# A spectral transformer block on one core: the forward transform's PSUM regions, its order of work and its weight planes rearranged

## The chip, the cores and the metric

The kernel runs on one core of one Trainium2 chip. TensorE (PE, with its weight loads as PEld) multiplies, VectorE (DVE) and ScalarE (ACT) read PSUM and work element by element, GpSimd (POOL) works on SBUF alone, and SyncE (SP) issues nearly all transfers. The metric is the device time of one execution in microseconds (us); the profiled execution has a time of its own and a span, from its first to its last instruction.

## The reference

One adaptive-norm block on x of 2048 tokens by 640 channels, bf16, batch 1:

```
mod = (silu(c) @ w_mod)                       # six rows of 640: sa ca ga sb cb gb
h = layernorm(x) * (1 + ca) + sa
x = x + ga * irfft2(rfft2(h) * (w_r + 1j*w_i))    # over tokens and channels
h = layernorm(x) * (1 + cb) + sb
x = x + gb * ((silu(h @ w_gate) * (h @ w_up)) @ w_down)   # hidden width 1728
```

## The kernel before

The 2D transform is done by matmuls. A token is 16p + t, with p one of 128 partitions and t one of 16 tiles; a channel is 5a + r, with r one of 5. The program has three parts, each with an order of steps written out as a string of short names; every engine runs its instructions in the order in which these steps issue them, and a scheduler adds only the waits. Tiles in PSUM come from pools of numbered buffers; a pool's next tile waits for the last reader of the buffer it takes. PSUM has eight banks, 512 fp32 columns each.

**Forward pass** (pool `ps1`, the plan "T0 T1 h0 ..."). For each of the 16 tiles: T transposes x in five 128x128 pieces into `t1ps` (L268); h copies them to `hT_all`, a ring of HB = 6 in SBUF (L271, on ACT but for tile 0); G multiplies each piece with itself and with two constant columns (+1/128, -1/128), so that the diagonal holds the sum of squares and two more columns hold the mean and its negative, in columns 320:450 of `t1ps` (L276); d reads those on DVE (L282 and its accumulator, then v, L284); m copies the negative mean to `negm` on ACT (L287); p and r make the reciprocal root for two tiles (L291 ACT, L295 DVE); s scales the token table Gtab by it (L300, L301, POOL; tile 15 on DVE); B multiplies `hT_all` with the channel table Rs into `zps` (L306); Z adds the mean's share, rv times `negm`, and copies to SBUF (L312, DVE); S multiplies Z with the scaled token table, four matmuls into `aps` (L320, L321); A copies that to `A_sb` (L327, ACT). `t1ps` has two buffers of one bank, `zps` one buffer of two banks, `aps` two of two banks. Ahead of this, `mod_ca` makes 1 + ca (25 one-column matmuls, L221, and an add, L337), which scales Rp into Rs (L341 on DVE for r = 0, 2, 4; L345 on ACT for 1, 3); rv is the column sum of Rs (L352) times 0.2 (L356, ACT). At its end `ms`, `sacs`, `mh`, `sh` make the transform of sa as `dsa` (L372 to L393).

**Middle stage** (pool `ps2`, four buffers of two banks, the plan "B4 B6 L0 Jn ..."). `A_sb` is cut in 17 units. Units 0 to 3 and 16 are transposed by TensorE (t2 L436, copy_t L442), the others by a DMA transpose on SP (L429, from B4 on). For each unit: X (stage_x, L456 to L464) is the short transform over the 16 tiles and the 5 channel residues, in which two matmuls of 5 rows, `first` with `dsa` (L459), add the share of sa; Xe copies it (L471, ACT); P multiplies with the spectral weights (L489, DVE, two instructions); Y transposes the products back (L503, L507) and y copies (L514, ACT or DVE); E is the inverse short transform (L530 to L538) and e copies to `Ep` (L548). The weights must be had in reversed order as well. For w_i this is a DRAM copy, `Wneg`, written by four DMAs (L198 to L201) and read back into `Wq` (L204). For w_r TensorE does it in two halves (turn_w: `jrev` L592, and the rows that wrap round by one-row matmuls of `identb`, L594), copied by ACT (L597). Jn, W and m negate parts on DVE (L254). `ga`, `gt`, `cb`, `sb` make the other rows of the modulation (L221 on PE); ga is spread over the partitions through DRAM (L236, L242) and multiplied into `Rinv_sb` (Ri, L585); L0 to L5 issue the later weights' DMAs (L602 to L616; Wu in L4, Wg in L5).

**Late stage.** The inverse pass (va L669, VT L676, dinv L682, x1 L685), the second norm, and the feed-forward (gu L774 and L761, silu L779, product L783, down projection L875 and L862, output L889).

Of the kernel before, what the change touches and what calls it, by code (L numbers as in the profile page):

```python
# [22 lines left out]
NC5 = 5  # L23
# [81 lines left out]
def adaln_block_kernel(  # L105
# [30 lines left out]
    one_p_ca = const.tile([P, NR], F32, name="one_p_ca")  # L136
# [5 lines left out]
    ssq, v25, rstd1, negm = (const.tile([P, NT], F32, name=n) for n in ("ssq", "v25", "rstd1", "negm"))  # L142
# [5 lines left out]
    dsa = const.tile([NR, 2, NR, 68], BF16, name="dsa")  # L148
    first = const.tile([NR, 128], BF16, name="first")
# [5 lines left out]
    HB = 6  # L155
# [20 lines left out]
    Wneg = dram.tile([P, NT, 2, 64], BF16, name="Wneg")  # L176
# [10 lines left out]
    nc.sync.dma_start(wm_ca, wm_v[:, :, D:2 * D])  # L187
    nc.sync.dma_start(Rp, R_dram)
    nc.sync.dma_start(x_sb[:, 2:4, :], x_v[:, 2:4, :])
    nc.sync.dma_start(Gtab[:, 0:4], G_dram[:, 0:4])  # L190

    for g in range(1, 4):
        nc.sync.dma_start(x_sb[:, 4 * g:4 * g + 4, :], x_v[:, 4 * g:4 * g + 4, :])
        nc.sync.dma_start(Gtab[:, 4 * g:4 * g + 4], G_dram[:, 4 * g:4 * g + 4])
    wv = A_w_i.rearrange("(k2 k1) l -> k2 k1 l", k1=P)[:, :, 64:320]
    to = Wneg[:].rearrange("k1 k2 m l -> k2 k1 m l")
    for m in range(2):
        nc.sync.dma_start(to[:, 1:128, m], wv[:, 127:0:-1, 128 * m:128 * m + 64])  # L198
    w0 = wv[:, 0].rearrange("k2 (m l) -> k2 m l", m=2)[:, :, 0:64]
    nc.sync.dma_start(to[0:15, 0], w0[1:16])  # L200
    nc.sync.dma_start(to[15:16, 0], w0[0:1])  # L201
    nc.sync.dma_start(wm_sa, wm_v[:, :, 0:D])
    nc.sync.dma_start(Wb[:, 0, :, 0:321], A_w_i.rearrange("(k2 k1) l -> k1 k2 l", k1=P))
    nc.sync.dma_start(Wqp[:, 2], Wneg[:].rearrange("k1 k2 m l -> k1 (k2 m l)"))  # L204
    nc.sync.dma_start(Ktab[:], K_dram)
    nc.sync.dma_start(Wb[:, 1, :, 0:321], A_w_r.rearrange("(k2 k1) l -> k1 k2 l", k1=P))
    nc.sync.dma_start(KIt[:], KI_dram)
    nc.gpsimd.memset(identb[:], 0.0)
# [4 lines left out]
                            pattern=[[1, 128]], channel_multiplier=1)  # L213
    nc.gpsimd.memset(first[:], 0.0)
    nc.gpsimd.memset(first[:, 0:1], float(S))
# [42 lines left out]
    with tc.tile_pool(name="ph1", bufs=3) as ph1, \  # L258
         tc.tile_pool(name="ps1", bufs=2, space=bass.MemoryType.PSUM) as ps1:
        t1s, zs, Zs, apss, Gss = {}, {}, {}, {}, {}  # L260
        ones = ph1.tile([P, 128], BF16, name="ones", bufs=1)
        nc.gpsimd.memset(ones[:], 1.0)

        def turn(t):
            t1s[t] = ps1.tile([P, 512], F32, name="t1ps", tag="t1")
            h = t1s[t][:, 0:320].bitcast(BF16).rearrange("p (r q) -> p r q", r=NR)
            for r in range(NR):
                nc.tensor.transpose(h[:, r, :], x_sb[:, t, r::NR], identb[:])  # L268

        def turned(t):  # L270
            (nc.vector.tensor_copy if t in HT_DVE else nc.scalar.copy)(  # L271
                hT_all[:, t % HB, :, 0:128], t1s[t][:, 0:320].bitcast(BF16).rearrange("p (r q) -> p r q", r=NR))

        def sums(t):
            for r in range(NR):
                nc.tensor.matmul(t1s[t][:, 320:450], lhsT=hT_all[:, t % HB, r, 0:128], rhs=hT_all[:, t % HB, r, 0:130],  # L276
                                 start=(r == 0), stop=(r == NR - 1))

        def stats(t):
            g = t1s[t][:, 320:450]  # L280
            junk = ph1.tile([P, 128], BF16, name="junk", bufs=2)
            nc.vector.tensor_tensor_reduce(out=junk[:], in0=g[:, 0:128], in1=identb[:], scale=25.0 / D, scalar=25.0 * EPS,  # L282
                                           op0=ALU.mult, op1=ALU.add, accum_out=ssq[:, t:t + 1])
            nc.vector.scalar_tensor_tensor(v25[:, t:t + 1], g[:, 128:129], g[:, 129:130], ssq[:, t:t + 1], ALU.mult, ALU.add)  # L284

        def mean(t):
            nc.scalar.copy(negm[:, t:t + 1], t1s[t][:, 449:450])  # L287
# [9 lines left out]
        def gscale(t):  # L297
            Gss[t] = ph1.tile([P, 3, 128], BF16, name="Gs", bufs=5)
            e = nc.vector if t in S_DVE else nc.gpsimd
            e.tensor_scalar(Gss[t][:, 0:2], Gtab[:, t], rstd1[:, t:t + 1], None, ALU.mult)  # L300
            e.tensor_scalar(Gss[t][:, 2], Gtab[:, t, 1], rstd1[:, t:t + 1], -1.0, ALU.mult, ALU.mult)  # L301

        def dfwd(t):
            zs[t] = ps1.tile([P, 2, 512], F32, name="zps", tag="z", bufs=1)
            for r in range(NR):
                nc.tensor.matmul(zs[t][:, r // 4, 128 * (r % 4):128 * (r % 4) + 128], lhsT=hT_all[:, t % HB, r, 0:128], rhs=Rs[:, r, :],  # L306
                                 start=True, stop=True)

        def zcopy(t):
            Zs[t] = ph1.tile([P, NR, 128], BF16, name="Z", bufs=4)  # L310
            z = zs.pop(t)
            nc.vector.scalar_tensor_tensor(Zs[t][:].rearrange("p r q -> p (r q)"), rv, negm[:, t:t + 1],  # L312
                                           z[:].rearrange("p b q -> p (b q)")[:, 0:D], ALU.mult, ALU.add)

        def s1(t):
            Z, Gs = Zs.pop(t), Gss.pop(t)
            apss[t] = ps1.tile([P, 2, 512], F32, name="aps", tag="a")
            for cc, a, b in ((0, 0, 2), (1, 1, 0)):
                o = apss[t][:, cc, 0:325].rearrange("p (r l) -> p r l", r=NR)
# [3 lines left out]
        def acopy(t):  # L323
            ap = apss.pop(t)
            o = A_sb[:, :, t, :, :]
            i = ap[:, :, 0:325].rearrange("p c (r l) -> p l c r", r=NR)
            (nc.vector.tensor_copy if t in A_DVE else nc.scalar.copy)(o, i)  # L327

        mpss = []

        def mod_ca(_):
            mpsA = ps1.tile([P, 2, 512], F32, name="mpsA", tag="a")
            mod_cols(mpsA[:, 0], wm_ca, strided=True)
            mpss.append(mpsA)

        def one_ca(_):
            nc.vector.tensor_scalar_add(one_p_ca[:], mpss[0][:, 0, 0:NR], 1.0)  # L337

        def rs_dve(_):
            for r in (0, 2, 4):  # L340
                nc.vector.tensor_scalar_mul(Rs[:, r, :], Rp[:, r, :], one_p_ca[:, r:r + 1])  # L341

        def rs_act(_):
            for r in (1, 3):
                nc.scalar.activation(Rs[:, r, :], Rp[:, r, :], ACT.Copy, scale=one_p_ca[:, r:r + 1])  # L345

        rvs = []

        def rv_mm(_):
            rvs.append(ps1.tile([P, 2, 512], F32, name="rvps", tag="a"))  # L350
            for b, w in ((0, 4), (1, 1)):
                nc.tensor.matmul(rvs[0][:, b, 0:128 * w], lhsT=ones[:], rhs=Rs[:, 4 * b:4 * b + w, :].rearrange("p r q -> p (r q)"),  # L352
                                 start=True, stop=True)

        def rv_out(_):
            nc.scalar.activation(rv, rvs[0][:].rearrange("p b q -> p (b q)")[:, 0:D], ACT.Copy, scale=0.2)  # L356

        cps = ps1.tile([P, 512], F32, name="cps", tag="t1")
        for k in range(NC5):
            nc.tensor.matmul(cps[:, k:k + 1], lhsT=c_row[0:1, k * 128:(k + 1) * 128], rhs=one11[:], start=True, stop=True)  # L360
        keep_warm(ps1, "t1", 12)
        nc.scalar.activation(sc_f[:], cps[:, 0:NC5], ACT.Silu)
# [3 lines left out]
        mps = []  # L366

        def mod_sa(q):
            if q == 0:
                mps.append(ps1.tile([P, 512], F32, name="mpsB", tag="t1"))  # L370
            for k in range(NC5):
                nc.tensor.matmul(mps[0][:, q:q + 1], lhsT=wm_sa[:, k, q:D:NR], rhs=sc_col[:, k:k + 1],  # L372
                                 start=(k == 0), stop=(k == NC5 - 1))

        def sa_cs(_):
            nc.vector.tensor_tensor(sacs[:], cs_v, mps[0][:, 0:NR].unsqueeze(2).to_broadcast([P, NR, 25]), ALU.mult)

        def mod_sahat(_):
            mps.append(ps1.tile([P, 512], F32, name="sps", tag="t1"))
            sv = sacs[:].rearrange("p r (f m) -> p r f m", f=5)  # L380
            for cc, a, b, e in ((0, 0, 1, 3), (1, 2, 0, 4)):
                o = mps[1][0:NR, 128 * cc:128 * cc + NL]
# [7 lines left out]
        def sa_out(_):  # L390
            sh = mps[1][0:NR, 0:256].rearrange("p (c l) -> p c l", c=2)[:, :, 0:NL].unsqueeze(2).to_broadcast([NR, 2, NR, NL])
            e5 = identb[0:NR, 0:NR].unsqueeze(1).unsqueeze(3).to_broadcast([NR, 2, NR, NL])
            nc.vector.tensor_tensor(dsa[:, :, :, 0:NL], sh, e5, ALU.mult)  # L393

        HT_DVE, A_DVE, S_DVE = (0,), (), (15,)
        GROUP = {0: 1, 1: 2, 3: 2, 5: 2, 7: 2, 9: 2, 11: 2, 13: 2, 15: 1}
        plan = (
            "T0 T1 h0 h1 G0 G1 d0 ca m0 d1 p0 r0 m1 oc rsD T2 rsA T3 h2 s0 rvp rv B0 h3 G2 G3 Z0 d2 B1 m2 p1 r1 d3 s1 m3 S0 "
            "T4 Z1 h4 G4 A0 T5 d4 s2 B2 h5 S1 Z2 m4 p3 G5 A1 T6 r3 d5 B3 s3 h6 S2 Z3 m5 G6 A2 T7 s4 d6 B4 h7 S3 Z4 m6 p5 G7 "
            "A3 T8 r5 d7 B5 s5 h8 S4 Z5 m7 G8 A4 T9 s6 d8 B6 h9 S5 Z6 m8 p7 G9 A5 T10 r7 d9 B7 s7 h10 S6 Z7 m9 G10 A6 T11 "  # L400
            "s8 d10 B8 h11 S7 Z8 m10 p9 G11 A7 T12 r9 d11 B9 s9 h12 S8 Z9 m11 G12 A8 T13 s10 d12 B10 h13 S9 Z10 m12 p11 G13 "
            "A9 T14 r11 d13 B11 s11 h14 S10 Z11 m13 G14 A10 T15 s12 d14 B12 h15 S11 Z12 m14 ms0 p13 G15 A11 ms1 r13 B13 d15 "
            "s13 ms2 ms3 Z13 m15 ms4 p15 S12 sacs s14 B14 r15 A12 s15 mh Z14 S13 B15 A13 S14 Z15 A14 S15 A15 sh "
        )
        steps = {"ca": mod_ca, "oc": one_ca, "rsD": rs_dve, "rsA": rs_act, "rvp": rv_mm, "rv": rv_out, "T": turn, "h": turned, "G": sums,
# [558 lines left out]
```

## Time and profile before

| | us |
|---|---|
| median of 3 runs | 281.07 (280.49 to 281.20) |
| the profiled execution, its own time | 280.74 |
| its span | 279.0 |
| PE busy | 266.0 (95%) |
| DVE busy | 149.8 (54%) |
| ACT busy | 125.2 (45%) |
| POOL busy | 21.2 (8%) |
| forward pass ends (last copy to `A_sb`) | 37.72 |
| inverse pass starts (first `va` matmul) | 79.25 |

Times in timelines and chains count from the span's start. A row of a timeline is: start, duration, engine, line, operation, result and operands, shape, count, and in brackets how long the engine had been idle and what ended that. Matmuls are pipelined, so a row's duration contains a tail that the next matmul overlaps: five 128-column matmuls in a row hold PE for about 0.28 us and read as 0.44.

### The profile page before, as it was taken

What the parts mean: (1) busy time and instruction counts of PE and PEld (TensorE: products, weight loads), DVE (VectorE), ACT (ScalarE), POOL (GpSimd) and SP (SyncE); (2) the same over time, 40 slices, a digit from 0 to 9 for tenths busy, and PEclk for the clock granted to TensorE, in tenths of its full rate; (3) what the DMA queues carried; (4) which work ended last, traced back from release to release, by engine and by line L of the source; (5) the groups of instructions that cost most, each with busy time, mean ns of one, the idle gap of its engine ahead of it and who ended that gap; (6) DMA issues with size and microseconds to landing.
All of it is one profiled execution on the core that took longest, in us unless ns stands there. A gap on an engine that the chain in (4) does not pass through costs nothing.

```text
span 279.0 us, 5360 instructions
## 1 busy us (share of the span) xinstructions
PE 266.0 (95%) x2191; PEld 166.3 (60%) x2191; DVE 149.8 (54%) x356; ACT 125.2 (45%) x239; POOL 21.2 (8%) x42
## 2 busy tenths in 40 slices
PE   6899989999996999999999999999999999999994
PEld 5677845787886665446654445664444674444663
DVE  2588856867858667896434534432325253422151
ACT  5699676877669996723022222203223203223000
POOL 2477710000000000000000000000000000000000
PEclk9999999999999999999999999999999999999999
DMA  7979949965599201005110004011002211000011
GB/s 248 356 151 362 308 82 197 329 210 178 175 318 367 74 9 34 1 0 96 47 56 5 9 0 94 12 61 33 12 0 40 57 71 33 12 0 0 0 49 47
DMA packets 38559, 28.84 MB, mean 103 GB/s; under 512 B 22022, under 2 KB 35591, under 8 KB 38407
## 3 DMA queue, kind: packets, MB, share of 16 engines
q1 hardware_dynamic: 38533, 28.50, 35.3%
q8 instruction: 17, 0.28, 0.4%
q14 instruction: 7, 0.06, 0.1%
q10 hardware_dynamic: 2, 0.00, 0.0%
HBM read 21.42 MB, written 3.15 MB: 88 GB/s over the span
## 4 chain that ended last, share of the span: by engine, by line
PE 83%; ACT 6%; DVE 4%; DMA 3%; issue 1%; SPq 0%; ACTq 0%; DVEq 0%
PE gu L774 40%; PE oa L875 20%; ACT early L271 3%; PE yps L503 2%; PE t1ps L276 2%; DMA x_sb<-in_A_x_dram 2%; PE va L669 2%; PE t1ps L268 2%; PE gu L761 2%; DVE late L685 1%; DMA ga_bc<-ga_row 1%; PE m_ps L221 1%; PE oa L862 1%; DVE PP L489 1%; PE oab L682 1%
## 5 line engine op out<-in xcount | busy, mean ns | idle before, releaser
L783 DVE TENSOR_TENSOR AT<-gu,sg 128x512 bf16<-128x512 f32 x52 | 35.9, 690 | 53.9 <-ACT sg L779 53.9
L774 PE MATMUL gu<-h2T_all,Wg 128*128 128x512 bf16 x260 | 64.6, 379 | 0.0
L774 PE MATMUL gu<-h2T_all,Wu 128*128 128x512 bf16 x260 | 64.6, 379 | 0.0
L779 ACT ACTIVATE sg<-gu 128x512 f32<-128x512 f32 x52 | 31.0, 596 | 70.1 <-PE gu L774 68.5
L875 PE MATMUL oa<-late,AT 128*128 128x320 bf16 x403 | 56.1, 299 | 0.0
L875 PEld LDWEIGHTS <-AT 128*128 128x128 bf16 x429 | 40.8, 98 | 17.2 <-issue 1.4
L774 PEld LDWEIGHTS <-Wu 128*128 128x128 bf16 x260 | 25.4, 98 | 30.7
L774 PEld LDWEIGHTS <-Wg 128*128 128x128 bf16 x260 | 25.1, 98 | 29.3
L889 DVE TENSOR_TENSOR xo<-oa,late 128x320 bf16<-128x320 f32 x31 | 20.0, 695 | 29.5 <-PE oa L862 16.3
L685 DVE SCALAR_TENSOR_TENSOR late<-oab,x_sb 128x640 bf16<-128x640 f32 x16 | 14.0, 884 | 9.4 <-PE oab L682 9.1
L763 ACT ACTIVATE sg<-gu 64x512 f32<-64x512 f32 x4 | 2.3, 586 | 34.9 <-PE gu L761 34.9
L312 DVE SCALAR_TENSOR_TENSOR Z<-rtile,negm,zps 128x640 bf16<-128x640 f32 x16 | 14.0, 876 | 2.6 <-ACT rtile L356 1.8
L300 POOL TENSOR_SCALAR Gs<-Gtab,rstd 128x256 bf16<-128x256 bf16 x15 | 13.8, 923 | 12.9 <-DMA Gtab<-tab_G 7.4
L693 ACT ACTIVATE junk<-late,mean 128x640 bf16<-128x640 bf16 x16 | 13.2, 827 | 0.3
L471 ACT CAST X<-xps 128x640 bf16<-128x640 f32 x16 | 11.2, 698 | 3.7 <-PE xps L464 2.5
L327 ACT CAST A_sb<-aps 128x650 bf16<-128x650 f32 x16 | 11.2, 702 | 2.6 <-PE aps L321 2.3
L503 PE MATMUL yps<-identb,PP 128*128 128x128 bf16 x130 | 10.2, 220 | 1.6 <-DVE PP L489 1.6
L669 PE MATMUL va<-Htab,Ep 128*128 128x128 bf16 x160 | 10.7, 219 | 0.7 <-ACT VT L676 0.4
L271 ACT COPY early<-t1ps 128x640 bf16<-128x640 bf16 x15 | 10.4, 692 | 1.9 <-PE t1ps L268 0.9
L676 ACT CAST VT<-va 128x640 bf16<-128x640 f32 x16 | 10.4, 700 | 1.4 <-PE va L669 1.4
L489 DVE TENSOR_TENSOR PP<-X,Wq 128x512 bf16<-128x512 bf16 x16 | 9.2, 575 | 2.5 <-ACT Wq L597 2.5
L669 PEld LDWEIGHTS <-Ep 128*128 128x128 bf16 x160 | 9.9, 118 | 0.9 <-issue 0.6
(288 smaller groups left out, 334.3 us busy)
## 6 DMA issues: line engine op xcount, KB each, us to landing
out_dram<-xo SPq DMA_DIRECT2D x15, 160.0 KB, 1.8
Wu<-in_B_w_up_dram SPq DMA_DIRECT2D x1, 2080.0 KB, 8.9
late<-in_B_w_down_dram SPq DMA_DIRECT2D x1, 2080.0 KB
x_sb<-in_A_x_dram SPq DMA_DIRECT2D x3, 640.0 KB, 9.6
early<-in_w_mod_dram SPq DMA_DIRECT2D x2, 800.0 KB, 4.8
wm_g<-in_w_mod_dram SPq DMA_DIRECT2D x2, 800.0 KB, 7.0
Wb<-in_A_w_i_dram SPq DMA_DIRECT2D x1, 1284.0 KB
Wb<-in_A_w_r_dram SPq DMA_DIRECT2D x1, 1284.0 KB, 10.7
```

What stands on the lines that cost most here:

```text
L271: (nc.vector.tensor_copy if t in HT_DVE else nc.scalar.copy)(hT_all[:, t % HB, :, 0:128], t1s[t][:, 0:320].bitcast(BF16).rearrange("p (r q ...
L300: e.tensor_scalar(Gss[t][:, 0:2], Gtab[:, t], rstd1[:, t:t + 1], None, ALU.mult)
L312: nc.vector.scalar_tensor_tensor(Zs[t][:].rearrange("p r q -> p (r q)"), rv, negm[:, t:t + 1], z[:].rearrange("p b q -> p (b q)")[:, 0:D], ...
L503: nc.tensor.matmul(yf[:, 128 * j:128 * j + 128], lhsT=PP[:, cp, 0:128] if u == 16 else PP[:, cp, 0:128, j], rhs=identb[:], start=(cp == 0) ...
L669: nc.tensor.matmul(vf[:, 128 * r:128 * r + 128], lhsT=Ep[:, t, 65 - 65 * g:193 - 65 * g, r], rhs=Htab[:, t, g, :], start=(f == 1 and r in ...
L685: nc.vector.scalar_tensor_tensor(x1[:, t, :].rearrange("p (r a) -> p r a", r=NR), VTs.pop(t).rearrange("p (r a) -> p r a", r=NR), 1.0, x_s ...
L693: nc.scalar.activation(junk[:], x1[:, t, :], ACT.Square, scale=-1.0, bias=mean2[:, t:t + 1], accum_out=sq2[:, t:t + 1])
L774: nc.tensor.matmul(o, lhsT=w_[:, c5, fc * 128:(fc + 1) * 128], rhs=h2T_all[:, sc % 2, :, c5, :], start=(c5 == 0), stop=(c5 == NC5 - 1))
L779: nc.scalar.activation(gus[fc][1][:], gus[fc][0][:, 0, :], ACT.Silu)
L783: nc.vector.tensor_tensor(AT[:, fc, :], gu[:, 1, :], sg[:], ALU.mult)
L875: nc.tensor.matmul(o, lhsT=AT[:, fc, tl * 128:(tl + 1) * 128], rhs=Wd_sb[:, fc, h * 320 + d0:h * 320 + d0 + n], start=(fc == 0 and not ear ...
L889: nc.vector.tensor_tensor(xos[tl][:, h * 320:(h + 1) * 320].rearrange("p (a r) -> p a r", r=NR), ps[0][0].rearrange("p (a r) -> p a r", r= ...
```

## The change

- The forward pass has four PSUM regions of two banks for its whole length, z0, z1, a0, a1, used by even and odd tiles. z holds the B product (columns 0:640) and, at 640:960, the transposed x; a holds the two halves of S (0:325 and 512:837), G's sums (382:512), and, at 838 and above, the small modulation products. `t1ps`, `zps`, `aps` are gone.
- m is gone: Z takes the negative mean from column 511 of a; v becomes a two-scalar instruction on PSUM columns.
- 1 + ca is summed in PSUM (a matmul of ones adds the 1), in two parts, k < 4 and k = 4, with `wm_ca`'s load split alike; Rs is scaled by five DVE instructions that take the scalar from PSUM. rv is copied in halves, by ACT and DVE.
- HB is 12, Gs has 6 buffers; p and r go by pairs from tile 0; POOL leaves tile 14 to DVE.
- x and Gtab are loaded two tiles at a time.
- `Wneg` is gone. Both planes are reversed by `jrev` in four pieces (J0 to J3, all 64 columns, 8 of the 16 k2 each); `jrev` has a one at (0, 0), and row 0 of `Wb` is overwritten with the wrapped rows by eight small DMAs. The copies are two on ACT, two on DVE.
- `first` and `dsa` have 128 rows, zero beyond the fifth, so the matmul that adds sa's share runs over 128 rows.
- copy_t of units 0 and 1 (not 2 and 3) is on DVE; y15 is on ACT.
- All orders of the first two parts are new. The late stage is the same.

The diff, cut:

```diff
-    HB = 6
+    HB = 12
-    for m in range(2):
-        nc.sync.dma_start(to[:, 1:128, m], wv[:, 127:0:-1, 128 * m:128 * m + 64])
...
+    for a in (1, 0):
+        nc.sync.dma_start(Wb[:, a, :, 0:321], ws[a])
...
+    for a in (1, 0):
+        for m in (65, 193):
+            for lo, hi, k in ((0, 15, 1), (15, 16, 0)):
+                nc.sync.dma_start(Wb[0:1, a, lo:hi, m:m + 63], ws[a][0:1, k:k + hi - lo, m:m + 63])
...
+        zf, af = [], []
+        for l, n in ((zf, "z0"), (zf, "z1"), (af, "a0"), (af, "a1")):
+            l.append(ps1.tile([P, 2, 512], F32, name=n + "ps", tag=n)[:].rearrange("p b q -> p (b q)"))
...
+        def turned_ps(t):
+            return zf[t % 2][:, 640:960].bitcast(BF16).rearrange("p (r q) -> p r q", r=NR)
...
-                nc.tensor.matmul(t1s[t][:, 320:450], lhsT=hT_all[:, t % HB, r, 0:128], rhs=hT_all[:, t % HB, r, 0:130],
+                nc.tensor.matmul(af[t % 2][:, 382:512], lhsT=hT_all[:, t % HB, r, 0:128], rhs=hT_all[:, t % HB, r, 0:130],
...
-            nc.vector.scalar_tensor_tensor(v25[:, t:t + 1], g[:, 128:129], g[:, 129:130], ssq[:, t:t + 1], ALU.mult, ALU.add)
-
-        def mean(t):
-            nc.scalar.copy(negm[:, t:t + 1], t1s[t][:, 449:450])
+            nc.vector.tensor_scalar(v25[:, t:t + 1], a[:, 510:511], a[:, 511:512], ssq[:, t:t + 1], ALU.mult, ALU.add)
...
-            nc.vector.scalar_tensor_tensor(Zs[t][:].rearrange("p r q -> p (r q)"), rv, negm[:, t:t + 1],
-                                           z[:].rearrange("p b q -> p (b q)")[:, 0:D], ALU.mult, ALU.add)
+            nc.vector.scalar_tensor_tensor(Zs[t][:].rearrange("p r q -> p (r q)"), rv, af[t % 2][:, 511:512],
+                                           zf[t % 2][:, 0:D], ALU.mult, ALU.add)
...
+        def r_scaled(_):
+            for r in range(NR):
+                nc.vector.tensor_scalar(Rs[:, r, :], Rp[:, r, :], ca_ps[:, r:r + 1], None, ALU.mult)
...
-            "T0 T1 h0 h1 G0 G1 d0 ca m0 d1 p0 r0 m1 oc rsD T2 rsA T3 h2 s0 rvp rv B0 h3 G2 G3 Z0 d2 B1 m2 p1 r1 d3 s1 m3 S0 "
-            "T4 Z1 h4 G4 A0 T5 d4 s2 B2 h5 S1 Z2 m4 p3 G5 A1 T6 r3 d5 B3 s3 h6 S2 Z3 m5 G6 A2 T7 s4 d6 B4 h7 S3 Z4 m6 p5 G7 "
...
+            "T0 T1 h0 G0 ca cb d0 h1 G1 T2 rs rvp h2 B0 rvA d1 p0 T3 rvD h3 B1 T4 h4 Z0 G2 B2 Z1 r0 T5 G3 T6 B3 d2 h5 T7 s0 "
+            "s1 Z2 d3 h6 B4 T8 h7 Z3 G4 S0 p2 r2 G5 d4 d5 S1 h8 T9 A0 s2 p4 T10 B5 Z4 r4 S2 A1 h9 s3 G6 s4 B6 S3 Z5 d6 G7 A2 "
+            "s5 Z6 d7 B7 A3 S4 h10 G8 T11 B8 Z7 p6 S5 B9 A4 h11 r6 T12 s6 Z8 d8 h12 G9 d9 T13 B10 G10 A5 Z9 S6 p8 A6 s7 ms0 "
+            "S7 r8 Z10 G11 T14 A7 B11 d10 ms1 h13 s8 B12 d11 G12 s9 S8 T15 Z11 p10 G13 r10 s10 B13 d12 h14 d13 ms2 h15 S9 A8 "
+            "Z12 p12 r12 ms3 A9 ms4 S10 G14 Z13 B14 sacs s11 S11 s12 A10 G15 d14 d15 A11 p14 B15 S12 Z14 s13 r14 s14 Z15 mh "
+            "S13 A12 s15 S14 A13 A14 S15 sh A15 "
...
-            for b in range(2):
-                nc.tensor.matmul(ps[:, b, :], lhsT=jrev[:], rhs=wv[:, 8 * b:8 * b + 8], start=True, stop=False)
-                for lo, hi, k in ((0, 8, 1),) if b == 0 else ((0, 7, 9), (7, 8, 0)):
-                    nc.tensor.matmul(ps[:, b, 64 * lo:64 * hi], lhsT=identb[0:1, :], rhs=wv[0:1, k:k + hi - lo], start=False, stop=k != 9)
+            for b in range(2):
+                nc.tensor.matmul(ps[:, b, :], lhsT=jrev[:], rhs=wv[:, 8 * (h % 2) + 4 * b:8 * (h % 2) + 4 * b + 4, :, 64:128], start=True, stop=True)
...
-            "B4 B6 L0 Jn T0 t0 T1 t1 T2 t2 J0 Je0 W0 X0 Xe0 T3 t3 W1 X1 Xe1 B8 L1 X2 Xe2 P0 X3 Xe3 B10 L2 Y0 P1 J1 y0 X4 "
...
+            "B4 B6 L0 W0 J3 T0 W1 T1 t0 J0 t1 Je3 J2 Je0 X0 Je2 Xe0 T2 T3 W2 Jn J1 t2 X1 B8 L1 t3 Je1 X2 X3 B10 L2 X4 Xe1 Xe2 "
+            "P0 P1 Y0 X5 B12 y0 Xe3 Xe4 P2 Y1 P3 X6 Xe5 y1 Xe6 E0 Y2 X7 B14 L3 e0 y2 Y3 Xe7 E1 y3 X8 P4 E2 P5 e1 Xe8 X9 e2 "
...
+            "Xe15 Y13 Y16 y13 E10 E11 y16 P15 Y14 e10 E12 e11 y14 e12 E13 e13 Y15 E16 y15 m1 E14 m2 e16 E15 e14 m3 e15 m4 sb "
+            "Ri cb L5 "
```

## The prediction

> **What bounds the kernel now.** I read the busy times by stage first, then the chain that ended last, then the timeline at the places that the change touches. The stages are cut where the forward pass ends (last A_sb copy, 37.72), where the inverse pass starts (first `va` matmul, 79.25) and where the feed-forward matmuls start. Columns: stretch, its length, then busy us and count of PE, PEld, DVE, ACT, POOL, the granted clock, the DMA share and GB/s.
> ```profile
> 0.00:37.72 37.72, 33.14 (x403) 25.78 (x404) 26.05 (x91) 27.75 (x64) 21.03 (x42) 1.00 0.83 264
> 37.72:79.25 41.53, 39.21 (x498) 29.99 (x498) 29.74 (x58) 29.63 (x52) 0.17 (x1) 1.00 0.81 210
> 79.25:94.20 14.95, 12.49 (x201) 11.56 (x202) 9.96 (x32) 13.65 (x26) 0.00 (x0) 1.00 0.91 315
> 94.20:279.00 184.80, 181.14 (x1090) 99.00 (x1088) 84.07 (x177) 54.16 (x98) 0.00 (x0) 1.00 0.12 29
> ```
> The last two stages are not edited and take 279.00 - 79.25 = 199.75 us. The change lives in the first two, 37.72 and 41.53 us. In the forward pass no engine is full; the chain of waits shows a loop:
> ```profile
> 22.21 0.69 ACT early L271
> 22.91 0.07 ACT negm L287
> 22.98 0.45 PE t1ps L276 x5
> 23.42 0.29 PE t1ps L268 x5
> ...
> 23.79 0.69 ACT early L271
> ```
> Copy h (L271), product sums G (L276), next transpose T (L268), next copy: 1.58 us a tile. The middle stage is PE's: 39.21 busy of 41.53.
>
> **Prices for the forward pass.** The end of that pass gives them:
> ```profile
> 35.31 0.88 DVE L312 SCALAR_TENSOR_TENSOR Z<-rtile,negm,zps 128x640 bf16<-128x640 f32 x1 [0.75 <-PE zps L306]
> ...
> 36.25 0.31 PE L320 MATMUL aps<-Z,Gs 128*128 128x325 bf16 x1 [0.42 <-DVE Z L312]
> ...
> 37.02 0.70 ACT L327 CAST A_sb<-aps 128x650 bf16<-128x650 f32 x1 [0.45 <-PE aps L321]
> ```
> Z takes 0.88 (the next DVE instruction follows 0.79 after its start), hands over in 0.06; S holds PE 0.56, and A starts 0.77 after S; A takes 0.70, h 0.69. A group of five transposes, sums or Z products holds PE 0.28, and its reader starts 0.45 to 0.48 after it does. The statistics d hold DVE 0.47; their last write is done at 0.56.
>
> **What the change removes there.** The mean copies m (16 x 0.164 = 2.6 us of ACT), the `t1ps` buffers and the single `zps`: T(t+2) no longer waits for m(t), and the loop above is gone. If nothing took its place, DVE would be next: Z 0.79, d 0.47 and half a reciprocal's 0.2 are 1.36 a tile.
>
> **What takes its place.** Everything of a tile's parity now lies in one z region (T, rv, Z products) and one a region (G, the sums with the mean, S, the `w_mod` columns). Two engines that use one region take turns, even where both only read. This case shows it:
> ```profile
> 11.26 0.22 DVE L284 SCALAR_TENSOR_TENSOR v<-t1ps,ssq 128x1 f32<-128x1 f32 x1
> ...
> 11.57 0.16 ACT L287 COPY negm<-t1ps 128x1 f32<-128x1 f32 x1 [0.89 <-DVE v L284]
> ```
> m needs nothing that v makes; both read `t1ps`, and ACT stands 0.89 us until v is done. The built order of the changed kernel carries such waits everywhere: A(t-4) waits for v(t), Z(t) for A(t-4), S(t-2) for Z(t), all by the a region; h(t+2) and Z(t), T(t+2) and Z(t) by the z region. So a region's round for two tiles is Z to S 0.94, S and G 0.84 with 0.2 to the reader, d 0.60, A 0.76: 3.34 us, **1.67 a tile** at best, against 1.58 now. The Trainium skill (PSUM — Partial Sum Buffer, "PSUM bank collisions raise a hardware error") says that two engines may not touch one bank and partition quadrant at once, reads against reads included, so the waits can't be shed. By that rule alone the region's second bank would be free for others, and the sa products before Z15 could start 0.9 us earlier than the built order lets them.
>
> I walked the built order, starting each instruction at the later of its engine's turn and its last releaser. PE is still at half pace in the first microseconds, as it is now:
> ```profile
> 7.57 1.26 PE L268 MATMUL t1ps<-identb,x_sb 128*128 128x128 bf16 x10
> ...
> 12.37 0.44 PE L268 MATMUL t1ps<-identb,x_sb 128*128 128x128 bf16 x5
> ```
> (5 in 0.56 + tail, then 5 in 0.28 + tail.)
> - Start. Rs is scaled by five DVE instructions (0.2 apart) instead of three beside two on ACT: done 8.95 instead of 8.4, about. rv by halves on ACT and DVE would be 0.3 shorter than its 0.70. But rvA (done 10.0) releases T3, T3 (0.74) releases rvD (0.4 by a proportion of rv's 0.70), rvD releases h3, h3 releases Z product 1 and behind it T4 (1.14 together, slow), T4 releases h4, and **Z0 waits for h4**: 14.05, where it is 10.14 now. x and G by pairs are not late for this: x tile 4 sits in the queue behind one G pair instead of two.
> - Z1 14.85. Z2 waits for T6, which stands in PE's queue behind T5, released by Z1: 18.05. Z3 waits for h7, behind T7, behind h5: 20.55. Z4 waits for T10 and A0: 23.95. Z5 waits for S3, which waits for A1: 26.8. Z6 28.95 (A2). Z7 31.2 (T11, A3). Z8 33.4 (T12, queued on PE behind S5, which waits for Z7). Z9 36.05 (A5). Z10 37.2 (A6). Z11 40.55 (T15, at the end of 3.0 us of PE work queued behind the A6 wait). Z12 43.6, Z13 44.55, Z14 47.8 (S12, behind A10, behind the sacs read of the same region), Z15 49.35. Three S and A in a row, taking turns, end at 53.2.
>
> That is 2.3 a tile instead of 1.67, because an order that suits one region leaves the other's turn waiting in an in-order queue. v as a two-scalar instruction saves at most 0.06 each (0.224 against 0.163 for the like row L698); Z's scalar from PSUM may cost the same 0.06; both are left at nothing. PE's pace may rise earlier than I assume (up to 2 us). I take **52.0**, plus 14.3; bounds 41 (the round's 3.34 kept from Z0 on: 14.05 + 7 x 3.34 + 1.0 + the 2.41 from Z15 to the end now = 40.8) and 58 (slow PE throughout).
>
> **The middle stage.** Per unit, PE spends 1.92 us (49.74 to 51.66): X 0.82, Y 0.55, E 0.55. In X:
> ```profile
> 49.87 0.30 PE L457 MATMUL xps<-Ktab,B2all 128*128 128x320 bf16 x1
> ...
> 50.10 0.11 PEld L459 LDWEIGHTS <-first 5*128 5x128 bf16 x2 [0.27 <-issue]
> ...
> 50.27 0.24 PE L461 MATMUL xps<-Ktab,B2all 128*128 128x160 bf16 x1
> ```
> L457's 320 columns end at 50.00; the two 5-row shifts then cost 0.27, nearly all of it the weight load's wait. Over 128 rows the nearest row is L221 (25 one-column matmuls in 0.96, 0.04 each): 0.08. So -0.19 x 16 = -3.0 (bounds 0 and -4.2, all idle time of L459). The four one-row matmuls of W go too: two half-planes cost 1.32 each, four new turns 4 x 0.43: -0.9, with the Wneg transfers, which nothing waits for now.
> Added: all four turned pieces must be copied before P0 (two by ACT at 1.01, two by DVE at about 1.2 by the 0.82 of L514), and the first turn waits for A15. P0 ends about 6.2 after A15. X4, ahead of Y0 in PE's queue, needs the first transposed block, 7.5 after its issue: Y0 at 8.2 instead of 43.45 - 37.72 = 5.7. From there PE has 16 x (0.55 + 0.55), 11 X x 0.64, three `w_mod` groups at 0.96 and 0.6 of small ones: 28.1. With stalls of 2 (2.3 now) the stage is 38.3: **-3.2** (bounds -5.2 and 0). The moved cb and Ri cost nothing more: cb is in the 28.1, Ri ran late behind its DMA (1.6 idle), and now d0 waits for it some 3 us after s0. Wg, now issued after cb (3.5 us later against s0), is first used 16 us after s0; 2.08 MB at the stage's 315 GB/s take 6.6.
>
> **Sum.** 52.0 + 38.3 + 199.75 = 290.1 of span, plus the 1.74 around it (280.74 - 279.00) = 291.8 against 280.74; the median of the three runs is 0.3 above that execution: **292**.
>
> **Rivals.**
> - A, forecast: 286.5 to 297. Chance 0.62.
> - B, the order packs better than my walk: the round's 1.67 a tile, forward 41 to 45, the middle's gain cancels it: 281 to 286, likeliest 283. For it: 3.34 is made of measured rows. Against: Z11's and Z14's waits are plain in the order. 0.18.
> - C, **faster**: turn-taking between readers costs little, and DVE's 1.36 decides: Z0 near 11, 15 x 1.36 + 0.9 for the odd work + 2.4 = 34.7, -3; with the middle 275. It decides if A and Z overlap in time on one region. Against: ACT's 0.89 above. It holds also if waits on the same region resolve earlier than I read them. 0.10.
> - D, PE stays at half pace through the forward pass, since its queue now has gaps: 0.84 more for S and G in each of 7 rounds: 298. The Trainium skill (TensorE: Matmul & The Clock Gate, "What's actually happening") has the full clock come after about 3.4 us of sustained activity; here it took from 3.76 to 11.8, so the trace is slower than that. 0.10.
>
> By cases: slower by over 0.3% (what a measurement here can tell from no change) 0.62 + 0.10 + 0.11 of B = 0.83; within 0.05; faster 0.02 + 0.10 = 0.12. The range 283 to 298 leaves out C and half of B's low side.
>
> **What would show it.** Z0 near 14; Z rows 1.7 to 3 us apart with DVE idle before them, ended by ACT A_sb or by PE; last A_sb copy ending near 52 (C: 35). L459's idle time gone; first Y near 8 after A15; `va` 38 after it. If `va` starts before 79 the forecast is wrong in the forward pass.

## The result and the profile after

The changed kernel takes 293.91 us (median of 4 runs, 292.83 to 295.04) against 280.93 before (280.49 to 281.20): ratio 1.0464, 95% interval 1.042 to 1.0508. It is slower, and the forecast was 292. Medians below are over all runs of a kernel; the ratios leave out three slow runs, two of ten in e5 and one of ten in e11.

First the busy times by stage of the changed kernel, cut as before at the last `A_sb` copy, the first `va` matmul and the feed-forward. Columns: stretch, its length, busy us and count of PE, PEld, DVE, ACT, POOL, granted clock, DMA share, GB/s.
```profile
0.00:55.55 55.55, 38.44 (x404) 30.52 (x404) 27.18 (x92) 25.09 (x45) 21.63 (x44) 0.94 0.49 161
55.55:92.20 36.65, 35.43 (x497) 30.93 (x497) 31.78 (x60) 29.30 (x53) 0.00 (x0) 1.00 0.86 223
92.20:107.15 14.95, 12.61 (x185) 12.10 (x185) 8.22 (x26) 12.76 (x24) 0.00 (x0) 0.89 0.96 346
107.15:293.20 186.05, 182.45 (x1109) 100.09 (x1106) 85.77 (x182) 55.56 (x101) 0.00 (x0) 1.00 0.11 30
```
The forward pass is 17.83 us longer (55.55 against 37.72) with nearly the same work on DVE and less on ACT. The middle is 4.88 shorter (36.65 against 41.53). What follows `va` is 201.0 instead of 199.75, with a granted clock of 0.89 at its start.

Where the forward pass stands still, in the waits of its first 55.55 us (engine, line, for whom: us in total, times, longest):
```profile
...
ACT A_sb L320 <- DVE v L285: 7.9, 5, 3.5
ACT early L273 <- PE z1ps L303: 7.7, 3, 4.4
DVE Z L308 <- PE z0ps L270: 5.3, 3, 2.4
DVE Z L308 <- ACT early L273: 4.7, 3, 2.8
```
The row above these is POOL's wait for the reciprocal roots (28.6); PE in its turn waited for POOL's scaled tables 3.1 in all. A copy A needs nothing that v makes; both only read the region. One such round, DVE and then ACT in the timeline, from Z5 on:
```profile
26.27 0.89 DVE L308 SCALAR_TENSOR_TENSOR Z<-rtile,a1ps,z1ps 128x640 bf16<-128x640 f32 x1 [1.92 <-PE a1ps L316]
...
27.41 0.28 DVE L285 TENSOR_SCALAR v<-a0ps,ssq 128x1 f32<-128x1 f32 x1
28.51 0.89 DVE L308 SCALAR_TENSOR_TENSOR Z<-rtile,a0ps,z0ps 128x640 bf16<-128x640 f32 x1 [0.82 <-ACT A_sb L320]
```
```profile
27.78 0.70 ACT L320 CAST A_sb<-a0ps 128x650 bf16<-128x650 f32 x1 [3.48 <-DVE v L285]
```
Z5 waits 1.92 for S3, which writes the same a1 region. Behind it in DVE's queue stands v6; for v6 on a0 stands A2 (3.48); for A2 stands Z6 (0.82). A turn on one region is handed to the other through an in-order queue.

A second cost shows in the row of granted clocks (40 slices of 7.3 us) and in three stretches of 3.4 us (columns as above):
```profile
PEclk9999797999998999999999999999999999999999
```
```profile
32.00:35.40 3.40, 3.16 (x24) 2.64 (x23) 1.17 (x4) 0.98 (x3) 2.51 (x4) 0.55 0.02 5
45.30:48.70 3.40, 3.36 (x20) 2.41 (x20) 1.59 (x6) 0.70 (x1) 2.52 (x4) 0.50 0.02 5
92.20:95.60 3.40, 3.40 (x40) 3.40 (x40) 0.00 (x0) 2.07 (x3) 0.00 (x0) 0.63 0.65 184
```
TensorE falls to half clock twice in the forward pass and once just after `va` begins. These stretches are cut a little off; in steps of 0.1 us each fall reads 0.50 for 3.41 us, from 31.61, 45.27 and 93.06. The profile of the kernel before shows none until its last microsecond.

The middle became shorter, as was said. The weight load of the shift, once 4.2 us idle over 16 units, has no idle time left (the line's instructions; nothing follows "until:"):
```profile
L449 PEld LDWEIGHTS <-first x32: 96/98/98, 57.8 to 83.3; 128*128 128x128 bf16 x32
```

### The profile page after: what moved, and what is told of

The parts are those of the page before. It is cut to its first block, busy times and chain, and to the rows that moved or that the text cites. A ratio compares the mean times of both kernels' runs of the same rounds, so it can differ in the third digit from the quotient of the medians.

```text
span 293.2 us, 5364 instructions
## 1 busy us (share of the span) xinstructions
PE 268.9 (92%) x2190; PEld 173.7 (59%) x2190; DVE 153.0 (52%) x358; ACT 122.7 (42%) x221; POOL 21.6 (7%) x44
## 4 chain that ended last, share of the span: by engine, by line
PE 83%; ACT 6%; DVE 6%; DMA 3%; issue 1%; DVEq 0%; ACTq 0%
PE gu L762 38%; PE oa L863 19%; DVE Z L308 2%; DMA B2all<-A_sb 2%; PE va L657 2%; ACT A_sb L320 2%; PE yps L493 2%; ACT early L273 2%; PE gu L749 1%; PE z0ps L303 1%; DVE late L673 1%; PE m_ps L219 1%; PE a1ps L315 1%; PE z0ps L270 1%; PE a0ps L277 1%
## 5 line engine op out<-in xcount | busy, mean ns | idle before, releaser
L877 DVE TENSOR_TENSOR xo<-oa,late 128x320 bf16<-128x320 f32 x31 | 20.0, 694 | 31.7 <-PE oa L850 18.6
L298 POOL TENSOR_SCALAR Gs<-Gtab,rstd 128x256 bf16<-128x256 bf16 x15 | 13.8, 923 | 30.5 <-DVE rstd L293 28.6
L657 PE MATMUL va<-Htab,Ep 128*128 128x128 bf16 x160 | 12.3, 238 | 0.8 <-ACT VT L664 0.4
L308 DVE SCALAR_TENSOR_TENSOR Z<-rtile,a0ps,z0ps 128x640 bf16<-128x640 f32 x8 | 7.1, 885 | 10.1 <-PE z0ps L270 5.3
L657 PEld LDWEIGHTS <-Ep 128*128 128x128 bf16 x160 | 11.4, 124 | 0.9 <-issue 0.8
L277 PEld LDWEIGHTS <-early 128*128 128x128 bf16 x80 | 7.0, 116 | 5.6 <-issue 4.5
L479 DVE TENSOR_TENSOR PP<-X,Wb 128x768 bf16<-128x768 bf16 x16 | 8.8, 551 | 2.3 <-ACT ga_col L559 1.9
L308 DVE SCALAR_TENSOR_TENSOR Z<-rtile,a1ps,z1ps 128x640 bf16<-128x640 f32 x8 | 7.0, 880 | 5.6 <-ACT early L273 1.9
```

The lines of the kernel that those rows point to most:

```text
L657: nc.tensor.matmul(vf[:, 128 * r:128 * r + 128], lhsT=Ep[:, t, 65 - 65 * g:193 - 65 * g, r], rhs=Htab[:, t, g, :], start=(f == 1 and r in ...
L877: nc.vector.tensor_tensor(xos[tl][:, h * 320:(h + 1) * 320].rearrange("p (a r) -> p a r", r=NR), ps[0][0].rearrange("p (a r) -> p a r", r= ...
```

## The experiments

Each row gives the median time, the interval of its ratio to runs of the kernel before on the same chip, and, from one profile, the end of the forward pass, the middle's length (to the first `va` matmul) and the rest of the span.

| kernel | us | ratio (95%) | forward | middle | rest |
|---|---|---|---|---|---|
| before | 280.93 | | 37.72 | 41.53 | 199.7 |
| changed | 293.91 | 1.042 to 1.051 | 55.55 | 36.65 | 201.0 |
| e1 old forward, new middle | 277.78 | 0.985 to 0.991 | 38.75 | 36.7 | 201.0 |
| e2 new forward, old middle | 298.42 | 1.059 to 1.064 | 53.76 | 41.5 | 199.3 |
| e3 mean from SBUF | 290.74 | 1.032 to 1.039 | 53.82 | 36.9 | 199.3 |
| e4 same regions, other order | 281.59 | 0.998 to 1.003 | 42.58 | 36.3 | 200.9 |
| e5 before + 128 rows | 282.40 | 0.999 to 1.006 | 37.76 | 42.5 | 199.8 |
| e6 e1 with 5 rows | 279.68 | 0.992 to 0.999 | 38.87 | 39.1 | 201.5 |
| e7 e1, cb earlier | 276.03 | 0.978 to 0.985 | 37.82 | 36.6 | 199.7 |
| e8 e7, other order on the old buffers | 276.18 | 0.978 to 0.985 | 36.91 | 36.5 | 199.8 |
| e9 e5, Ri last | 277.53 | 0.985 to 0.990 | 38.90 | 37.9 | 199.8 |
| e10 changed, h4 behind Z0 | 293.55 | 1.041 to 1.049 | 53.22 | 36.5 | 201.4 |
| e11 before, loads by pairs | 281.27 | 0.998 to 1.003 | 38.67 | 41.5 | 199.7 |
| e12 e4, cb earlier | 280.66 | 0.998 to 1.003 | 42.86 | 36.2 | 199.4 |

**e1 and e2, the two halves apart.** e1 has the regions, order and x and G loads of before and everything else of the change; e2 is the complement.

> Forward pass of the kernel before (its regions, order, and x and G loads), with the changed middle stage (shift over 128 rows, both W planes turned on TensorE, new order). Changed kernel: va starts 36.65 us after the last A_sb copy, against 41.53 before, so 4.9 less; its part behind va is 1.25 longer (201.0 against 199.75). Theory (the edits of the middle are a gain by themselves): last A_sb copy near 37.7, va 36.6 to 38.3 later (38.3 is the forecast of record), total 276 to 278. Rival (the middle gains only because a slow forward pass lets its loads land early): the middle waits for the W planes, and gains under 2: 279 or more. If the 1.25 behind va belongs to the middle's order, it shows here too.

> The complement: the changed forward pass (regions held twice, its order, x and G by pairs) with the middle stage of before. Theory (all the loss is in the forward pass): last A_sb copy near 55.5 (before 37.72), middle 41.5, total 281 + 17.8 = 298 to 299. Rival (part of the loss comes from the changed middle or its loads): under 296.

Measured 277.78 and 298.42. The middle's edits gain with the old forward pass too (middle 36.7), and the forward pass loses with the old middle. e2's profile kept a granted clock of 1.00 throughout, and its forward pass ended at 53.76: by these two profiles, an estimate, the half clock in the changed kernel's cost about 2 us of the 17.83, and most of the 17.83 is there without it. Over the runs the clock does not order the times: e2's other run with a mean of 1.00 took 298.42, 2 us more than the profiled one. The rest behind `va` is 201.0 in e1 and 199.3 in e2: the 1.25 us comes with the changed middle, not with the forward pass, though not in every execution (e3, below, has the changed middle and 199.3).

**e3, Z out of the a region.**
```diff
+            nc.vector.tensor_copy(negm[:, t:t + 1], a[:, 511:512])
...
-            nc.vector.scalar_tensor_tensor(Zs[t][:].rearrange("p r q -> p (r q)"), rv, af[t % 2][:, 511:512],
+            nc.vector.scalar_tensor_tensor(Zs[t][:].rearrange("p r q -> p (r q)"), rv, negm[:, t:t + 1],
```
The order also moves d8 and d10 ahead of their Z.

> The changed kernel with one edit in the forward pass: DVE copies the negative mean from the a region to SBUF behind v (16 small copies), and Z takes it from there; d8 and d10 move ahead of their Z. Z then uses the z region only, and its turn in the a region (Z after A(t-4), S(t-2) after Z) is gone. Theory (turns between engines on one region, in this order, make the loss): my walk of the order with measured durations gives a forward pass 4 us shorter, 51.5, total 289 to 291. Rival (PE's half pace and late transposes set the time, the turn costs nothing): the sixteen copies cost DVE up to 2 us, total 294 or more.

Measured 290.74, 3.2 less than the changed kernel, although DVE does sixteen more copies. The rival falls: taking one user out of the region, with the two moves, gains; the moves were not run alone. How much of it is the turns is not settled: in the profile the forward pass ends at 53.82, only 1.7 earlier where the walk said 4, with one fall of the clock in it instead of two, and another 1.7 lies behind `va`, where the clock stays at 1.00. The three other runs took 290.3 to 290.8 with a mean clock of 0.970, lower than the profiled run's 0.994 (292.17), so fewer falls do not explain the median. A, d, G and S still share the region.

**e4, the same regions in another order.** Only the forward pass's order string differs; it begins and goes on:
```diff
-            "T0 T1 h0 G0 ca cb d0 h1 G1 T2 rs rvp h2 B0 rvA d1 p0 T3 rvD h3 B1 T4 h4 Z0 G2 B2 Z1 r0 T5 G3 T6 B3 d2 h5 T7 s0 "
...
+            "T0 h0 T1 T2 h1 ca cb h2 rs T3 G0 rvp rvD h3 rvA T4 d0 B0 Z0 G1 B1 d1 Z1 p0 r0 B2 h4 G2 B3 G3 T5 d2 Z2 d3 s0 p2 "
+            "Z3 T6 h6 G4 r2 s1 S0 B4 d4 h5 S1 s2 G5 Z4 B5 T7 d5 A0 p4 s3 T8 h8 S2 Z5 G6 B6 h7 B7 A1 r4 Z6 T9 S3 s5 G7 h9 d6 "
...
```


> The changed kernel with the same regions, instructions and middle stage, but another order of the forward pass, looked for with the turns on the regions counted. Theory (the order is what loses, the regions alone cost little): walked with the measured durations the last A_sb copy ends at 40.6 (PE at half pace to 14 us) to 42.6 (to 18.6), total 279 to 282. Rival (the regions themselves are the loss: with one user of a region at a time no order gets under 2.3 us a tile): last A_sb copy past 50, total 289 or more. Second rival (the PE falls back to half pace in any order of this kind): 44 to 47.

Measured 281.59, forward pass 42.58. The same instructions on the same regions are 12.3 us faster. The A copies' waits for v are down from 7.9 us to 1.7 (three, the longest 1.2). PE also comes to full pace earlier (groups of five read 0.44 or 0.45 from 13.99 on, from 18.62 in the changed kernel), and the clock does not fall in this forward pass; the shares of the three in the 12.3 were not separated. Z's in e4, after the start:
```profile
15.41 0.88 DVE L308 SCALAR_TENSOR_TENSOR Z<-rtile,a0ps,z0ps 128x640 bf16<-128x640 f32 x1
16.73 0.88 DVE L308 SCALAR_TENSOR_TENSOR Z<-rtile,a1ps,z1ps 128x640 bf16<-128x640 f32 x1
18.23 0.89 DVE L308 SCALAR_TENSOR_TENSOR Z<-rtile,a0ps,z0ps 128x640 bf16<-128x640 f32 x1
19.62 0.89 DVE L308 SCALAR_TENSOR_TENSOR Z<-rtile,a1ps,z1ps 128x640 bf16<-128x640 f32 x1
```
They stand 1.3 to 1.5 us apart here; from Z0 at 12.69 to Z15 at 38.69 the mean is 1.73 (25.17 / 15 = 1.68 before, 38.05 / 15 = 2.54 in the changed kernel).

**e12, what the regions cost in their better order.** e4 with e7's middle.

> The changed kernel with both orders mended: the forward pass in the order looked for with the turns counted, and cb in the middle behind E13's copy. Against the run with the old buffers in their best order (276.2) it has the same middle stage, so the difference is what the regions held twice cost when the order suits them. Theory (the round's 3.34 us for two tiles, 0.1 a tile over the old loop, and a start that is later by the turns): last A_sb copy 40.6 to 42.6 against 36.9, total 279.5 to 281. Rival (the regions cost nothing in a right order, the rest is PE's later warm-up): under 278.

Measured 280.66, against 276.03 and 276.18 for the old buffers with the same middle. So the rearranged forward pass costs some 4.5 us even in the better order. In the profiles (e7's against this one's) it ends 5.0 later: 2.7 of that is there when Z0 starts (12.96 instead of 10.30), 0.9 comes from Z0 to Z15, 1.5 behind Z15. How much of the start is the regions' turns, and how much the other edits there (Rs by five instructions, rv in halves), was not separated. That it is the best order for the regions is not shown.

**e10, one early wait.**
```diff
-            ... h3 B1 T4 h4 Z0 G2 ...
+            ... h3 B1 Z0 T4 h4 G2 ...
```


> The changed kernel with T4 and h4 moved behind Z0 in the order of the forward pass, nothing else. Theory (Z0 waits for h4, as the forecast has it, but the later turns of the order take most of it back): Z0 at 11.0 instead of 13.5, the last A_sb copy 1.3 to 1.4 us earlier by the walk, total 292 to 293. Rival (the late start is carried through whole): 2.9 us less, 291.

Z0 starts at 11.50 instead of 13.53, so it was h4 that it waited for. The median is only 0.4 us below the changed kernel's (293.55), half a microsecond above what was expected, and the intervals overlap. The forward pass ends 2.3 earlier in the profile, but there with one fall of the clock ahead of its end instead of two (at 42.91). Of the 2 us at the start at most a part comes through; how much is not settled by these runs.

**e5 and e9, the shift over 128 rows alone.** e5 makes `first` and `dsa` 128 rows deep in the kernel before; e9 also moves Ri from behind y8 to the end of the middle's order.

> The kernel before with one edit: first and dsa take 128 rows (123 of them zero), so the two shift products of a unit load full weights. Theory (the forecast's term): the weight load's idle time before L459 (16 x 0.26 = 4.2 us) goes, 0.19 a unit or 3.0 us shorter in a stage that PE bounds, total 278 (277 to 279). Rival (the time goes to the next late thing, or the 123 added rows cost as much): above 280.

Measured 282.40: no gain, where 3 us were expected (the two runs with a mean clock of 1.000 took 279.52 and 280.36). The DVE timeline of the kernel before and of e5 says why:
```profile
64.64 0.49 DVE L585 TENSOR_TENSOR Rinv_sb<-Rinv_sb,ga_bc 128x640 bf16<-128x640 bf16 x1 [1.60 <-DMA ga_bc<-ga_row]
```
```profile
64.63 0.49 DVE L586 TENSOR_TENSOR Rinv_sb<-Rinv_sb,ga_bc 128x640 bf16<-128x640 bf16 x1 [3.44 <-DMA ga_bc<-ga_row]
```
Ri starts at the same moment in both, when the gate row's transfer has landed; e5 only came to it 1.84 us earlier. PE then waited 2.8 us for the product queued behind Ri, and ran at half clock from 66.22, for 3.41 us (e5, stretches of 2 us):
```profile
64.00:66.00 2.00, 0.00 (x0) 0.00 (x0) 1.37 (x3) 0.35 (x1) 0.00 (x0) 1.00 0.88 206
66.00:68.00 2.00, 1.85 (x15) 1.63 (x16) 2.00 (x5) 0.00 (x0) 0.00 (x0) 0.55 1.01 403
```


> The kernel before with the shift over 128 rows, and one step of the middle's order moved: Ri (DVE scales Rinv by the gate row) to the end, as in the changed kernel. With the rows alone DVE stood 3.44 us at Ri, until the gate row's transfer was there at 64.63 (before: 1.60, until 64.64), PE stood 2.8 behind it, and its granted clock fell to 0.55 to 0.59 from 66 to 70 us. Theory (the rows save their 3 us, and Ri's wait for its transfer took them back): va 3 to 4 us earlier than in the run with the rows alone, no such fall, total 277 to 278.5. Rival (the rows save little, the wait only shows spare time): above 280.

Measured 277.53, middle 37.9: 3.3 less than before. The rows are worth something like their 3 us once Ri no longer waits in their way; what Ri's move gives without the rows was not run.

**e6, the new middle with 5 rows.** e1 with `first` and `dsa` as before.

> The kernel with the forward pass of before and the changed middle stage, but with the shift over 5 rows as before. Theory: the W planes on TensorE and the new order give the smaller part of the middle's 4.9 us, the rows 3.0: 3 us slower than the same kernel with 128 rows (277.8), 280 to 281.5, near the kernel before. Rival (the order and the planes are the gain): under 279.

Measured 279.68: 1.9 more than e1, less than the 3.0 expected. The medians mix two kinds of execution, though: e1's four runs all have a mean clock of 0.993 or 0.994, of e6's ten five have 0.988 to 0.994 (280.1 to 281.4 us) and five 0.999 or 1.000 (277.7 to 279.3). The two profiled executions, with one fall each, differ by 3.0 (281.31 against 278.35), 2.4 of it in the middle's length (39.1 against 36.7). So the rows are worth about 3 where like is compared with like, as expected; the rest of the middle's gain is left to the planes and the order.

**e7 and e8, a version that beats both.**
```diff
-            ... E13 e13 Y15 ... m4 sb Ri cb L5 "
+            ... E13 e13 cb L5 Y15 ... m4 sb Ri "
```


> The kernel with the forward pass of before and the changed middle stage (277.8), with one step of the middle's order moved: cb (25 one-column products of w_mod and its copies) and the Wg loads behind it go from the end to behind E13's copy, as before. At the end PE now waits 0.33 for a copy of cb before va, and its granted clock falls to 0.72 just behind (76 to 80 us), with 201.0 us from va to the end against 199.7 before. Theory (cb at the end costs): va 0.3 to 1.0 earlier, and without the fall 1.3 less behind it: 275.5 to 277. Rival (the fall comes from elsewhere, and cb only fills PE's time at the end): 277.3 or more.

Measured 276.03, 1.75 less than e1. Behind `va`, e1 and then e7 (the same matmuls; x38 and x62 done in 3.5 us):
```profile
75.40:78.90 3.50, 3.43 (x38) 3.43 (x38) 0.00 (x0) 1.65 (x4) 0.00 (x0) 0.59 0.62 163
```
```profile
74.30:77.80 3.50, 3.40 (x62) 3.49 (x62) 0.73 (x3) 2.56 (x6) 0.00 (x0) 1.00 1.04 375
```
In e1 PE goes from 50 one-column products in a row (2.2 us) through a 0.33 us gap into `va`; its clock falls at 74.84, within the second 25 and ahead of the gap. In e7, with 25 of them there, it does not fall. One fall takes 0.006 off an execution's mean clock (an estimate: half of 3.41 us in 276): e1's four runs have 0.993 or 0.994, e7's five 0.999 or 1.000. cb at the end makes the fall likely, not certain: e3's profile has cb there and none behind `va`, and of e4's ten runs six have 0.994 (281.6 to 283.3 us) and four 1.000 (280.1 to 280.8).

> The kernel of the run with cb earlier, and the forward pass in another order on its old buffers (m, G, d and A of a tile moved against each other; nothing else). Walked with the measured durations the last A_sb copy ends 1.1 us earlier than in the order of before (36.6 against 37.7). Theory (the forward pass is a matter of order): 1 us below the run with cb earlier, 274.5 to 276. Rival (the old order is already at its loop of 1.58 us a tile): no difference.

Measured 276.18: the forward pass ends 0.9 earlier in the profile, and the median shows nothing of it (275.0 to 276.9). A miss: either the executions vary more than the gain, or part of it is lost later; not settled. Both kernels are about 1.8% faster than the kernel before.

**e11, the loads alone.** x, Gtab and the first part of `w_mod` in the changed kernel's pieces.

> The kernel before with the loads of the changed one: x and G by pairs of tiles in alternation, and w_mod's first part in two pieces. Theory (no tile is late for it, and none gains): Z2 at 14.7, last A_sb copy at 37.7, total within 0.5 of before. Rival (the loads set the start): Z2 later by 0.5 us or more.

Measured 281.27, no difference. Z2 came at 15.62, 0.9 late in this one profile, but so it did in e1 and e9 (15.71, 15.85) with the old loads.

## Why the prediction was right, and where it was not

The profiled execution was 293.2 of span; the sum had 290.1. By its steps:

- **Turns on a region: right.** e3 takes one user away and gains 3.2 us, and in e4 the waits go with the order. The Trainium skill (PSUM — Partial Sum Buffer, "PSUM bank collisions raise a hardware error") asks for them; here they are waits that the scheduler puts in, over both banks of a region: the sa products, which write a0's second bank, waited 0.98 us (at 50.87) for Z14, which reads only its first. No run left the turns out.
- **The order keeps the regions from their round: right.** 1.67 a tile was said to be the best, and e4 reaches 1.73. Rival B's 283 is thus the price of the regions in a better order (e4 281.59), and the changed order does not reach it.
- **The walk: right, and then set aside.** Measured less walked, the Z's stand at -0.5 for Z0, -0.7 to -0.4 up to Z7, +0.7 to +0.9 from Z8 to Z13, and +2.1 and +2.2 for Z14 and Z15; the end at +2.35 (55.55, walk 53.2). The two steps of 1.2 and 1.4 lie at the two falls of the clock, at 31.61 and 45.27. In e2, which has none, Z8 to Z15 are within 0.45 of the walk, and the end is 53.76. So rival D came true in part, beside the forecast. "I take 52.0", because PE's pace might rise earlier than walked, was the wrong choice: groups of five still took 0.74 at 17.10, and 0.44 only from 18.62 on. This term was 3.55 too small: 1.2 by that choice, about 1.8 by the falls if e2's profile stands for the pass without them, 0.56 by the walk.
- **The middle: right in kind, 1.65 too small a gain.** "Y0 at 8.2": the first Y started 6.46 after the last `A_sb` copy, because X4 could start at 61.38, 5.75 after its block's transfer was issued (55.63), without a wait: the 7.5 from issue to landing was the median of six such transfers, and the first was quicker.
- **"The moved cb and Ri cost nothing more": wrong, both ways.** Moving Ri gains 4.9 once the rows are there (e5 against e9); moving cb costs 1.75 (e7 against e1), 1.3 of it behind `va`, where the clock falls in e1.
- **"The last two stages are not edited": true, yet 1.25 longer.** Behind the moved cb they run 3.41 us at half clock in this execution; e7, with cb back, has 199.7, and e3 199.3, where cb is moved and the clock does not fall.
- **v**: the two-scalar form takes 0.28 instead of 0.22, not less. Sixteen times 0.06 on an engine that is idle half of the pass (busy 27.18 of 55.55).
- x and G by pairs: nothing, as said (e11).

The errors, +3.55 - 1.65 + 1.25, make the 3.15 between the sum (290.05 before rounding) and the profiled span; the median of the runs is 1.1 below that execution. That the forecast came within 1.9 of the median owes something to luck: the middle's larger gain hides a third of what the forward pass and the falls added.

## What to carry to other kernels

Before two engines are given one PSUM region, count its users in turn, and look in the in-order queues for what stands between two turns: the rearranged forward pass cost some 4.5 us here, the order on top of it some 12. When a bound engine is made faster, look at the next wait with a fixed end, such as a transfer: it takes the gain, and an engine that then stands idle may come back at half clock. An order found for one set of costs must be looked for again when a turn or a duration changes.

## What the runs showed of the hardware that was not expected

- TensorE's granted clock falls to exactly half for a fixed time: each of the ten falls that lie whole within the fourteen profiles reads 0.50 for 3.41 us (three more begin in the last microsecond of a span). In the changed kernel they begin at 31.61, 45.27 and 93.06, which is 4 and 14 steps of 3.41 apart, and e10's two (42.91, 90.70) lie 14 steps apart. In the step ahead of each PE was busy for 1.53, 2.13 and 3.08 us, the last mostly with one-column products. The Trainium skill (TensorE: Matmul & The Clock Gate, "What's actually happening") has the throttled state come after an idle window of about 3.4 us; the length and the depth of the falls agree, but no window ahead of these three was idle. The busy time alone does not decide: steps with 1.93 (from 35.03) and 1.99 (from 52.09) brought no fall, and e2 had PE busy for 1.52 of 3.4 us from 28.4 and kept 1.00. What decides is not shown.
- The half pace at the start is not in the granted clock: 1.00 over 3.6 to 18.6 us of the changed kernel, where a group of five matmuls holds PE for 0.53 instead of 0.28. In the kernel before it lasted from the first products, at 2.25 and not from 3.76 as the prediction counts, to 11.8. It must be read from the matmuls.
